# A long convolution beside a gated feed-forward layer: the convolution's transforms taken as two blocks of 1024 time steps

## The chip, the cores and the metric

The kernel runs on one core of one Trainium2 chip. The metric is the device time of one launch in microseconds (us). The engines are called PE (TensorE, matrix products), DVE (VectorE), ACT (ScalarE), POOL (GpSimd) and SP (SyncE, which here only issues DMAs).

## The reference

All inputs are bfloat16. `A_q`, `A_k`, `A_v` and the output are [1, 2048, 512] (time steps by channels), `ssm_k` is [512, 2048], `shift_k` [512, 4], the feed-forward weights are 512x1792, 512x1792 and 1792x512.

```python
def _A_ref(q, k, v, shift_k, ssm_k, ssm_D):
    ...                                   # k_shift: causal convolution of k with 4 taps for each channel
    kv = k_shift * v
    ...                                   # y: causal convolution of kv with ssm_k along time, 2048 steps, by FFTs of 4096
    y = y + kv * ssm_D[None, None, :]
    return q * y

def _B_ref(x, w_gate, w_up, w_down):
    h = _gelu(x @ w_gate) * (x @ w_up)
    return h @ w_down

x = A_q
xn = _layernorm(x, axis=-1)
s = _A_ref(xn, A_k, A_v, A_shift_k, A_ssm_k, A_ssm_D)
g = _silu(_B_ref(xn, B_w_gate, B_w_up, B_w_down))
return x + s * g
```

(`@` stands for the reference's einsums.)

## The kernel before

**Layout.** Partition p holds the time steps 16p to 16p+15; a tile t is one of the 16 steps, 128 partitions by 512 channels. The feed-forward part runs over four quarters q of four tiles. In a quarter, `unit(q, m)` computes for each of 14 chunks of 128 hidden columns four products for the gate (`g`) and four for the up projection (`u`), 512 wide, then Gelu on ACT (`GE`, L1072) and the product on DVE (`HT`, L1075). `down(q)` multiplies back: 14 products for each tile, in tasks of 4, 5 and 5; for quarters 0 to 2 the result becomes tanh-based silu in `G` (L1099, L1101), for quarter 3 it goes straight to the output (L1107 to L1110).

**The convolution.** It is done by transforms in several stages through DRAM scratch `ZH`, `ZK`, `ZI`:

- *First stage* (`stage1`, matrix `F1`): a transform along the 128 partitions. `x="H"` takes the filter `ssm_k` (transposed on PE before, `h_transpose`, L863; `ssm_D` is added to its first step), `x="K"` takes `kv` (in `V`). For each of the 16 tiles there are two products of 128 rows by 128 columns, 512 wide (real and imaginary part, `c`). Two such tiles go to one `AST` buffer (evicted by ACT or DVE, L593 or L596) and are stored to `ZH` or `ZK`.
- *Second stage* (`fwd`): the scratch is read back as 32 groups of 128 rows, four groups to a load of 512 KB (`BH`, `BK`). For each such load `tiles` issues 16 products of 32x32, at row and column positions 0, 32, 64 and 96, 512 wide, into four banks (L963). One is a "pass" below. H's results go to `HS`, and SP's swap DMAs make `HW` from it with even and odd partitions exchanged; K's go to `KB`.
- *Product and inverse* (`spectrum`): DVE multiplies `KB` into `HS` and `HW` in place (L1026, 1024 columns each, four for each load), and the inverse (`MI`) of the second stage is two passes that accumulate, one on `HS`, one on `HW`. The results go to `BO` and are stored to `ZI` from ACT's queue.
- *Last stage* (`y`): `ZI` is read back as 8 loads `BI`; for each there are four products with `G1`, 128 rows by 128 columns, 512 wide. DVE then multiplies with `XN` and `G` (L1146, L1152).

The matrices are made at the start from integer phases by the Sin function (L705), products of tables on DVE (L699, L702), sign changes on ACT (`m_turn`, L714) and three DMA transposes.

**Order.** All work is a list of tasks with numbers in the order in which `S.add` is called. `SEQ` is a written-out order of these numbers; a "b" behind a number takes the second engine offered (an eviction on DVE instead of ACT). `Sched.run` walks through `SEQ` and gives out buffers and PSUM banks by a model of durations; then each engine's instructions are issued in that order, and `Trk` puts in the semaphore waits. PSUM has 8 banks: `pF` gives out single banks to the feed-forward products (four at most), `pC` pairs of banks to the convolution. PE takes its products strictly in the order of `SEQ`.

The call for the small tiles, and the helper for the full ones:

```python
trk.op("PE", lambda h: h.matmul(ps(s, i)[b, :], lhsT=wt(col)[a, :], rhs=data(col)[a, :], start=n < 16, stop=n >= len(todo) - 16, tile_position=(32 * row, 32 * col)),
       r=rt, w=[R_ps[s][i]], accum=True, quiet=n < len(todo) - 1)

def mm(h, o, l, r, st, sp):
    return h.matmul(o, lhsT=l, rhs=r, start=st, stop=sp)
```

Of the kernel before, what the change touches and what calls it, by code (L numbers as in the profile page):

```python
# [6 lines left out]
BF16 = mybir.dt.bfloat16  # L7
# [7 lines left out]
DM = 512  # L15
# [5 lines left out]
NG = 32  # L21
# [34 lines left out]
T_INV = 438.0  # L56
# [335 lines left out]
def build_kernel(nc, A_q, A_k, A_v, A_shift_k, A_ssm_k, A_ssm_D, B_w_gate, B_w_up, B_w_down, out):  # L392
    with ExitStack() as es0:
# [23 lines left out]
        TFB = at("TFB", [128, NG, 32], BF16, place["at"] + 2048)  # L417
# [11 lines left out]
        SKB = new("SKB", [128, 4, DM], BF16)  # L429
        Drow = new("Drow", [1, DM], BF16)  # L430
# [22 lines left out]
        C32 = at("C32", [128, 2, 128], I32, xnT_at + 0)  # L453
        K32 = at("K32", [128, 128], I32, xnT_at + 1024)
        K4 = at("K4", [128, 128], I32, xnT_at + 1536)
# [9 lines left out]
        HW = [new(f"HW{j}", [128, 4, DM], BF16) for j in range(3)]  # L465
        HS.append(new("HS2", [128, 4, DM], BF16))
        KB = new("KB", [128, 4, 2, DM], BF16)
        BO = new("BO", [128, 4, 2, DM], BF16)
# [529 lines left out]
        for n in range(8):  # L998
            h_stage2(n)
# [222 lines left out]
```

## Time and profile before

| | |
|---|---|
| Median of 3 runs | 199.13 us (198.84 to 199.38) |
| Span of the profiled execution, first to last instruction | 197.8 us |
| PE busy | 191.3 us (97%), granted clock 0.999 |
| DVE, ACT, POOL busy | 161.5 us (82%), 119.5 us (60%), 12.2 us (6%) |
| PE products of the first stage: `V,F` and `HTr,F` | 32 and 32, 128\*128, 512 wide |
| PE products of the last stage: `BI,G` | 32, 128\*128, 512 wide |
| PE products of 32\*32: `BH`, `BK`, `HS`, `HW` | 128 each |
| DVE products of the spectrum (L1026) | 32 |

The span is the time between the first and the last instruction of one profiled execution; the time of a run is measured around it and is 1.3 us longer here. Durations of instructions overlap on an engine, so a product that is listed with 379 ns can start 216 ns after the one before it. In a line of groups the columns are line, engine, operation, out<-in, shape, count, then busy us and mean ns, then idle time before them and what ended it.

### The profile page before, as it was taken

The page shows a single profiled execution, that of the slowest core. Times are in us where ns is not written, and L with a number is a line of the kernel's source. Part 1 is how long each engine was busy: PE and PEld are TensorE (multiplying, and loading weights), DVE is VectorE, ACT ScalarE, POOL GpSimd, SP SyncE. Part 2 cuts the span into 40 slices and gives each one's busy share as a digit, 9 for nine tenths or more (in the row PEclk, how much of TensorE's full clock was granted, in tenths as well). Part 3 has the DMA queues.
Part 4 walks back from the last instruction along what each step waited for, and adds up shares of the span by engine and source line. Part 5 has one row for each costly group of instructions (what it writes and reads, how often), then busy time and mean ns, then how long its engine had stood idle before and what let it go on. Part 6 is the DMA issues. An engine that isn't in the chain of part 4 may idle for free.

```text
span 197.8 us, 3488 instructions
## 1 busy us (share of the span) xinstructions
PE 191.3 (97%) x1380; PEld 87.1 (44%) x1380; DVE 161.5 (82%) x247; ACT 119.5 (60%) x160; POOL 12.2 (6%) x26
## 2 busy tenths in 40 slices
PE   7989999899999999999999999999999999999993
PEld 2656644344444444443444333443344444444542
DVE  6687899888999898889589795897895765878994
ACT  4494877585978768875756958846754453330111
POOL 7300800000000000020200000000000000000000
PEclk9999999999999999999999999999999999999999
DMA  5999999999576849798999963994415133956363
GB/s 126 332 303 347 372 375 391 383 418 210 173 311 274 275 95 381 251 342 267 289 257 218 331 236 126 319 367 148 162 53 215 48 120 100 374 162 195 122 247 126
DMA packets 36870, 48.66 MB, mean 246 GB/s; under 512 B 10483, under 2 KB 29815, under 8 KB 36854
## 3 DMA queue, kind: packets, MB, share of 16 engines
q1 hardware_dynamic: 31350, 40.05, 64.0%
q10 hardware_dynamic: 5504, 8.39, 11.4%
q8 instruction: 11, 0.18, 0.4%
q14 instruction: 5, 0.04, 0.1%
HBM read 27.39 MB, written 14.68 MB: 213 GB/s over the span
## 4 chain that ended last, share of the span: by engine, by line
PE 89%; DMA 5%; SPq 2%; DVE 1%; issue 0%; ACT 0%
PE psall L602 83%; PE psall L963 5%; DMA Wu<-in_B_w_up_dram 5%; SPq L574 2%; PE psall L863 1%; DVE KTM L944 1%; DVE G L1109 0%; DVE G L1110 0%; ACT G L1107 0%
## 5 line engine op out<-in xcount | busy, mean ns | idle before, releaser
L602 PE MATMUL psall<-xnT,Wg 128*128 128x512 bf16 (+1 forms) x232 | 55.8, 372 | 1.7 <-DMA Wg<-in_B_w_gate_dram 1.0
L602 PE MATMUL psall<-xnT,Wu 128*128 128x512 bf16 (+1 forms) x232 | 55.3, 372 | 0.2 <-DMA Wu<-in_B_w_up_dram 0.2
L602 PE MATMUL psall<-Wd,HT 128*128 128x512 bf16 (+1 forms) x238 | 53.2, 367 | 0.0
L1075 DVE TENSOR_TENSOR HT<-psall,GE 128x512 bf16<-128x512 f32 x54 | 36.5, 686 | 10.1 <-PE psall L602 7.5
L1072 ACT ACTIVATE GE<-psall 128x512 bf16<-128x512 f32 x54 | 30.8, 599 | 14.0 <-PE psall L602 11.4
L602 PEld LDWEIGHTS psall<-xnT,Wg 128*128 128x128 bf16 x232 | 22.1, 98 | 27.6 <-ACT GE L1063 1.4
L602 PEld LDWEIGHTS psall<-Wd,HT 128*128 128x128 bf16 x238 | 22.6, 98 | 25.8 <-issue 1.9
L602 PEld LDWEIGHTS psall<-xnT,Wu 128*128 128x128 bf16 x232 | 21.8, 98 | 27.2 <-issue 2.2
L593 ACT ACTIVATE HS<-psall 128x1024 bf16<-128x1024 f32 x15 | 14.6, 1021 | 6.7 <-PE psall L963 6.7
L593 ACT ACTIVATE KB<-psall 128x1024 bf16<-128x1024 f32 x10 | 10.1, 1024 | 8.9 <-PE psall L963 8.9
L946 DVE TENSOR_TENSOR KAC<-KAC,KTM 128x2048 bf16<-128x2048 bf16 x12 | 14.6, 1218 | 0.1
L944 DVE TENSOR_TENSOR KTM<-KK,SKB 128x2048 bf16<-128x2048 bf16 x12 | 14.6, 1217 | 0.0
L593 ACT ACTIVATE AST<-psall 128x1024 bf16<-128x1024 f32 x12 | 11.9, 1022 | 2.5 <-PE psall L602 2.4
L596 DVE CAST BO<-psall 128x1024 bf16<-128x1024 f32 x7 | 8.6, 1223 | 5.6 <-PE psall L963 5.6
L1026 DVE TENSOR_TENSOR HS<-KB,HS 128x1024 bf16<-128x1024 bf16 x16 | 10.9, 684 | 1.6 <-ACT KB L593 1.6
L1099 ACT ACTIVATE G<-psall 128x512 bf16<-128x512 f32 x12 | 7.2, 601 | 8.2 <-PE psall L602 7.8
L1107 ACT ACTIVATE G<-psall 128x512 bf16<-128x512 f32 (+1 forms) x5 | 2.5, 511 | 15.9 <-PE psall L602 15.9
L593 ACT ACTIVATE BO<-psall 128x1024 bf16<-128x1024 f32 x9 | 9.1, 1024 | 4.8 <-PE psall L963 4.6
L806 DVE BATCH_NORM_STATS2 stats<-X 128x6 f32<-128x512 bf16 x16 | 10.5, 679 | 1.2 <-DMA X<-in_A_q_dram 1.0
L815 POOL TENSOR_TENSOR mv<-mv,NHALF 128x4 f32<-128x4 f32 (+1 forms) x5 | 5.9, 1176 | 83.8 <-DVE mv L814 83.8
L1026 DVE TENSOR_TENSOR HW<-KB,HW 128x1024 bf16<-128x1024 bf16 x16 | 10.9, 684 | 0.0
L596 DVE CAST KB<-psall 128x1024 bf16<-128x1024 f32 x6 | 7.3, 1223 | 3.6 <-PE psall L963 3.4
(79 smaller groups left out, 179.3 us busy)
## 6 DMA issues: line engine op xcount, KB each, us to landing
BH<-ZH SPq DMA_DIRECT2D x8, 512.0 KB, 5.1
HW<-HS SPq DMA_DIRECT2D x16, 256.0 KB, 3.8
BK<-ZK SPq DMA_DIRECT2D x8, 512.0 KB, 6.1
ZI<-BO ACTq DMA_DIRECT2D x16, 256.0 KB, 3.4
BI<-ZI SPq DMA_DIRECT2D x8, 512.0 KB, 4.5
ZK<-AST SPq DMA_DIRECT2D x6, 512.0 KB, 3.6
Hn<-in_A_ssm_k_dram SPq DMA_DIRECT2D x4, 512.0 KB, 7.9
KK<-in_A_k_dram SPq DMA_DIRECT2D x4, 512.0 KB, 11.9
```

What stands on the lines that cost most here:

```text
L593: return h.activation(o, i, ACTF.Copy, scale=scale)
L596: return h.tensor_copy(o, i)
L602: return h.matmul(o, lhsT=l, rhs=r, start=st, stop=sp)
L806: t_stats[t] = op([("DVE", 670.0)], lambda e, h, t=t: h.bn_stats(stats[:, t, :], X[:, t, :]), r=[bX[q][t % 4]], w=[bst[t]], rr=[R_X[t]], w ...
L815: t_pw = op([("POOL", 850.0)], lambda e, hd, ts=ts, n=n: hd.tensor_tensor(mv[:, ts, 3:4], mv[:, ts, 2:3], NHALF[:, 0:n, :], ALU.pow), r=[b ...
L944: op([("DVE", dur)], lambda e, h, j=j, m=m: h.tensor_tensor(KTM[:, m.slot, :, :], kk(j), sk(j), ALU.mult), r=need + [bSKB[j], a], w=[m], r ...
L946: op([("DVE", dur)], lambda e, h, m=m: h.tensor_tensor(KAC[:, a.slot, :, :], KAC[:, a.slot, :, :], KTM[:, m.slot, :, :], ALU.add), r=[m], ...
L963: trk.op("PE", lambda h: h.matmul(ps(s, i)[b, :], lhsT=wt(col)[a, :], rhs=data(col)[a, :], start=n < 16, stop=n >= len(todo) - 16, tile_po ...
L1026: return hd.tensor_tensor(o, flat(KB, kb[h]), o, ALU.mult)
L1072: op([("ACT", act(512))], lambda e, h: h.activation(GE[:, g.slot, :], bank(pg), ACTF.Gelu_apprx_tanh), r=[pg], w=[g], rr=lambda: R_bank(pg ...
L1075: op([("DVE", dve(512, 1))], lambda e, h: h.tensor_tensor(HT[:, q % 2, m, :], bank(pu), GE[:, g.slot, :], ALU.mult), r=[pu, g], w=[bHT[q][m]],
L1099: op([("ACT", act(n))], lambda e, h, g=g, pc=pc: h.activation(g, pc(), ACTF.Tanh, scale=0.5), r=[p], w=[bt], rr=lambda p=p: R_bank(p), ww= ...
```

## The change

The convolution of 2048 steps becomes one of two blocks of 1024 (`NB = 2`): block 0 of the output takes block 0 of both inputs; block 1 takes K's block 0 times the filter's second spectrum plus K's block 1 times the filter's first. Each block has 16 groups (`NG = 16`), so that the scratch has 32 groups as before.

- `F1` and `G1` shrink to [128, 128]. K's first stage is one task for two tiles with four products of 64 rows, at row positions 0 and 64. H's first stage has, for each tile, one product of the first 64 rows and one of all 128. The last stage is one task for two loads with eight products of 64 columns, at column positions 0 and 64.
- The forward passes stay 16. The inverses are four of two passes (block 0) and four of four passes (block 1).
- DVE's products of the spectrum are 12 for each pair of loads: four in place on the filter's second spectrum, four into `KB` buffers, four in place on its first; 48 in all.
- Scratch rows lie in runs of two tiles (2 KB) instead of four. The tables `TF`, `TFA`, `TFB`, `MI` have half the size. `HW` and `HS` have four buffers each, `KB` six, `BO` and the third `BK` lie elsewhere.
- `SEQ` is new as a whole. Of its entries, evictions on DVE: before, 7 of `BO`, 6 of `KB`, one of `HS`, one of `HTr`, two of `xnT`; after, 5 of `BO`, 2 of `KB`, two of `xnT`. The first loads on SP's queue: before `x0` (four), `h0`, `h1`, `wg0`, `x1`, `wg1`, `wu0`, the bulk of the halo of k, `h2`, `wu1`, `h3`; after `x0` (four), `h0`, `h1`, `wu0`, `wg0`, `x1`, `wg1`, the halo, `wu1`, `h3`, and `h2` five loads later. (`D0`, 1 KB, stands among the `x0`.)

Cut to its core, without `SEQ`, phases of the tables and pools:

```diff
-NG = 32
+NG = 16
+NB = 2
...
-        F1 = new("F1", [128, 2, 128], BF16)
-        G1 = new("G1", [128, 2, 128], BF16)
+        F1 = new("F1", [128, 128], BF16)
+        G1 = new("G1", [128, 128], BF16)
...
-        MI = new("MI", [128, 2, 8, 128], BF16)
+        MI = new("MI", [128, 2, NG // 4, 128], BF16)
         def stage1(x, u, Z):
             a = B(f"A{x}{u}", pAST[x])
             af = [] if x == "H" else s1_tasks["H"] + kshift_tasks[:1] + [t_table]
+            pp = [B(f"ps1{x}{u}_{i}", pC) for i in range(2)]
+            if x == "K":
+                def halves(e):
+                    for i in range(2):
+                        for b in range(2):
+                            k = slice(64 * b, 64 * b + 64)
+                            trk.op("PE", lambda h, i=i, b=b, k=k: h.matmul(ps(psl(pp[i]), b), lhsT=F1[k, :], rhs=V[k, 2 * u + i, :], start=True, stop=True, tile_position=(64 * b, 0)),
+                                   r=[R_F1, R_V[2 * u + i]], w=[R_ps[psl(pp[i])][b]], accum=True)
+                s1_tasks[x].append(S.add([("PE", 2 * T_FWD)], halves, r=[bF1, bKV[u // 2]], w=pp, lat=200.0, mode=2))
             for i in range(2):
-                p = B(f"ps1{x}{u}_{i}", pC)
+                p = pp[i]
                 data, rd, bd = (HTr[:, u, 512 * i:512 * i + 512], R_HTr[u], [bHTr[k][u // 4] for k in (2 * i, 2 * i + 1)] + ([bFold] if u == 0 else [])) if x == "H" else (V[:, 2 * u + i, :], R_V[2 * u + i], [bKV[u // 2]])
 
                 def m(e, p=p, data=data, rd=rd):
                     s = psl(p)
-                    for c in range(2):
-                        trk.op("PE", lambda h, c=c: mm(h, ps(s, c), F1[:, c, :], data, True, True), r=[R_F1, rd], w=[R_ps[s][c]], accum=True)
-                s1_tasks[x].append(S.add([("PE", pe(2))], m, r=[bF1] + bd, w=[p], lat=200.0))
+                    for b, k in ((0, 64), (1, 128)):
+                        trk.op("PE", lambda h, b=b, k=k: mm(h, ps(s, b), F1[0:k, :], data[0:k], True, True), r=[R_F1, rd], w=[R_ps[s][b]], accum=True)
+                if x == "H":
+                    s1_tasks[x].append(S.add([("PE", pe(2))], m, r=[bF1] + bd, w=[p], lat=200.0))
 
                 def ev(e, h, p=p, i=i):
                     if x == "K":
-                        return copy(e, h, ast[x][a.slot][:, i, :, :].rearrange("p c d -> p (c d)"), ps(psl(p)))
-                    return copy(e, h, ast[x][a.slot][:, :, :, 256 * i:256 * i + 256], ps(psl(p)).rearrange("p (c d r) -> p r c d", c=2, r=2))
+                        return copy(e, h, ast[x][a.slot][:, :, i, :], ps(psl(p)).rearrange("p (b d) -> p b d", b=2))
+                    return copy(e, h, ast[x][a.slot][:, :, :, 256 * i:256 * i + 256], ps(psl(p)).rearrange("p (b d r) -> p b r d", b=2, r=2))
                 op(EV(1024), ev, r=[p], w=[a], rr=lambda p=p: R_ps[psl(p)], ww=lambda: [R_AST[x][a.slot]], after=af)
 
             def st(e):
-                dst = bass.AP(Z, 4 * u * DM, [[32 * DM, 128], [DM, 4], [1, DM]])
-                dma(e, dst, ast[x][a.slot].rearrange("p r c d -> p (r c) d"), d_ast[x][a.slot], [R_AST[x][a.slot]], [R_Z[x][u]])
+                dst = bass.AP(Z, 2 * u * DM, [[16 * DM, 128], [NG * 128 * DM, NB], [DM, 2], [1, DM]])
+                dma(e, dst, ast[x][a.slot], d_ast[x][a.slot], [R_AST[x][a.slot]], [R_Z[x][u]])
             t_st = S.add([("ACT", 350.0) if x == "H" else ("SP", ISSUE)], st, r=[a], w=[bZ[x][u]], nbytes=1.9 * SMALL if x == "H" else W_ZK)
             (zh_tasks if x == "H" else zk_tasks).append(t_st)
 
...
-            return lambda e: tiles(pp, [(lambda c: TF[:, 4 * n + c, :], lambda c: T[:, buf.slot, c, :], [R_MF, R_T[buf.slot]])])
+            return lambda e: tiles(pp, [(lambda c: TF[:, 4 * (n % 4) + c, :], lambda c: T[:, buf.slot, c, :], [R_MF, R_T[buf.slot]])])
...
-        for out_ap, in_ap, rr, ww, rb, wb in ((G1[:], F1[:].rearrange("p c k -> p (c k)"), R_F1, R_G1, bF1, bG1), (MI[:, 0, :, :], TFA[:].rearrange("p g j -> p (g j)"), R_MFA, R_MI[0], bMF2, bMI[0]),
+        for out_ap, in_ap, rr, ww, rb, wb in ((G1[:], F1[:], R_F1, R_G1, bF1, bG1), (MI[:, 0, :, :], TFA[:].rearrange("p g j -> p (g j)"), R_MFA, R_MI[0], bMF2, bMI[0]),
...
-                op(EV(1024), lambda e, hd, p=p, h=h: copy(e, hd, HS[hs.slot][:, 2 * h:2 * h + 2, :].rearrange("p c d -> p (c d)"), ps(psl(p)), 2.0 ** -12),
-                   r=[p], w=[hs], rr=lambda p=p: R_ps[psl(p)], ww=lambda h=h: [R_HS[hs.slot][h]], after=g1_tasks + (kshift_tasks if n >= 2 else []))
+                op(EV(1024), lambda e, hd, p=p, h=h: copy(e, hd, HS[hs.slot][:, 2 * h:2 * h + 2, :].rearrange("p c d -> p (c d)"), ps(psl(p)), 2.0 ** -11),
+                   r=[p], w=[hs], rr=lambda p=p: R_ps[psl(p)], ww=lambda h=h: [R_HS[hs.slot][h]], after=g1_tasks + (kshift_tasks if n not in (0, 4) else []))
...
-        for n in range(8):
+        for n in (0, 4, 1, 5, 2, 6, 3, 7):
...
-        t_inv = []
...
-        def spectrum(n):
-            bk, hs, hw = B(f"bk{n}", pBK), bHS[n], bHW[n]
-            pk, pi = ([B(f"ps{x}{n}_{h}", pC) for h in range(2)] for x in "ki")
-            kb, bo = ([B(f"{x}{n}_{h}", p) for h in range(2)] for x, p in (("kb", pKB), ("bo", pBO)))
-            S.add([("SP", ISSUE)], lambda e: dma(e, BK[:, bk.slot, :, :], z_rows(ZK, 4 * n, 4), d_bk[bk.slot], R_Z["K"], [R_BK[bk.slot]]),
+        def kload(n):
+            bk = B(f"bk{n}", pBK)
+            S.add([("SP", ISSUE)], lambda e: dma(e, BK[bk.slot][:], z_rows(ZK, 4 * n, 4), d_bk[bk.slot], R_Z["K"], [R_BK[bk.slot]]),
...
-
-            S.add([("PE", T_FWD)], fwd(pk, BK, R_BK, bk, n), r=[bMF, bk], w=pk, lat=200.0, mode=1)
+            return bk
+
+        def kspec(n, bk):
+            pk, kb = ([B(f"{x}{n}_{h}", p) for h in range(2)] for x, p in (("psk", pC), ("kb", pKB)))
+            S.add([("PE", T_FWD)], lambda e: tiles(pk, [(lambda c: TF[:, 4 * (n % 4) + c, :], lambda c: BK[bk.slot][:, c, :], [R_MF, R_BK[bk.slot]])]), r=[bMF, bk], w=pk, lat=200.0, mode=1)
...
-                for b, T, R_o in ((hs, HS, lambda h=h: [R_HS[hs.slot][h]]), (hw, HW, lambda h=h: R_HW[hw.slot][h])):
-                    def mul(e, hd, h=h, b=b, T=T):
-                        o = T[b.slot][:, 2 * h:2 * h + 2, :].rearrange("p c d -> p (c d)")
-                        return hd.tensor_tensor(o, flat(KB, kb[h]), o, ALU.mult)
-                    op([("DVE", dve(1024, 2))], mul, r=[kb[h], hs, hw], w=[b], rr=lambda h=h, R_o=R_o: [R_KB[kb[h].slot]] + R_o(), ww=R_o)
+            return kb
+
+        def half(T, b, h):
+            return T[b.slot][:, 2 * h:2 * h + 2, :].rearrange("p c d -> p (c d)")
+
+        def inverse(s, b, terms):
+            n = 4 * b + s
+            pi, bo = ([B(f"{x}{n}_{h}", p) for h in range(2)] for x, p in (("psi", pC), ("bo", pBO)))
...
-                tiles(pi, [(lambda c, m=m: MI[:, m, n, 32 * c:32 * c + 32], lambda c, T=T, b=b: T[b.slot][:, c, :], [R_MI[m], *R_b])
-                           for m, T, b, R_b in ((0, HS, hs, R_HS[hs.slot]), (1, HW, hw, sum(R_HW[hw.slot], [])))])
-            t_inv.append(S.add([("PE", T_INV)], inv, r=[*bMI, hs, hw], w=pi, lat=200.0, mode=1))
+                tiles(pi, [(lambda c, m=m: MI[:, m, s, 32 * c:32 * c + 32], data, [R_MI[m], *rb()]) for m, data, rb, _ in terms])
+            S.add([("PE", T_FWD * len(terms))], inv, r=[*bMI, *[x for t in terms for x in t[3]]], w=pi, lat=200.0, mode=1)
...
-        for n in range(8):
-            spectrum(n)
+        def spectrum(s):
+            (h0, w0), (h1, w1) = ((bHS[n], bHW[n]) for n in (s, 4 + s))
+            bk0 = kload(s)
+            kb0 = kspec(s, bk0)
+            bt = [B(f"kt{s}_{h}", pKB) for h in range(2)]
+
+            def mul(h, kb, b, T, o, ob, R_i, R_o):
+                op([("DVE", dve(1024, 2))], lambda e, hd: hd.tensor_tensor(o(), flat(KB, kb[h]), half(T, b, h), ALU.mult), r=[kb[h], b, ob], w=[ob],
+                   rr=lambda: [R_KB[kb[h].slot]] + R_i(), ww=R_o)
+
+            def r_hs(b, h):
+                return lambda: [R_HS[b.slot][h]]
+
+            def r_hw(b, h):
+                return lambda: R_HW[b.slot][h]
+
+            def r_kb(b):
+                return lambda: [R_KB[b.slot]]
+
+            def in_place(kb, hs, hw):
+                for h in range(2):
+                    mul(h, kb, hs, HS, lambda h=h: half(HS, hs, h), hs, r_hs(hs, h), r_hs(hs, h))
+                    mul(h, kb, hw, HW, lambda h=h: half(HW, hw, h), hw, r_hw(hw, h), r_hw(hw, h))
+            in_place(kb0, h1, w1)
+            for h in range(2):
+                mul(h, kb0, h0, HS, lambda h=h: flat(KB, bt[h]), bt[h], r_hs(h0, h), r_kb(bt[h]))
+                mul(h, kb0, w0, HW, lambda h=h: flat(KB, kb0[h]), kb0[h], r_hw(w0, h), r_kb(kb0[h]))
+
+            def kb_term(m, b):
+                return m, lambda c: KB[:, b[c // 2].slot, c % 2, :], lambda: [R_KB[x.slot] for x in b], b
+
+            def h_term(m, T, b, R):
+                return m, lambda c: T[b.slot][:, c, :], R, [b]
+            inverse(s, 0, [kb_term(0, bt), kb_term(1, kb0)])
+            kb1 = kspec(4 + s, kload(4 + s))
+            in_place(kb1, h0, w0)
+            inverse(s, 1, [h_term(m, T, b, R) for hs, hw in ((h1, w1), (h0, w0))
+                           for m, T, b, R in ((0, HS, hs, lambda hs=hs: R_HS[hs.slot]), (1, HW, hw, lambda hw=hw: sum(R_HW[hw.slot], [])))])
+
+        for s in range(4):
+            spectrum(s)
...
+        p_y = [B(f"psy{j}", pC) for j in range(8)]
+        b_bi = [B(f"bi{j}", pBI) for j in range(8)]
...
-            p = B(f"psy{j}", pC)
-            bi = B(f"bi{j}", pBI)
+            p, bi = p_y[j], b_bi[j]
...
-                src = bass.AP(ZI, 4 * j * DM, [[32 * DM, 128], [DM, 4], [1, DM]])
-                dma(e, BI[:, bi.slot, :, :], src, d_bi[bi.slot], R_Z["I"], [R_BI[bi.slot]])
+                src = bass.AP(ZI, 2 * j * DM, [[16 * DM, 128], [NG * 128 * DM, NB], [DM, 2], [1, DM]])
+                dma(e, BI[:, bi.slot, :, :].rearrange("p (b t) d -> p b t d", b=NB), src, d_bi[bi.slot], R_Z["I"], [R_BI[bi.slot]])
...
-
-            def y(e, bi=bi, p=p):
-                s = psl(p)
-                for i in range(2):
-                    for c in range(2):
-                        trk.op("PE", lambda h, i=i, c=c: mm(h, ps(s, i), G1[:, c, :], BI[:, bi.slot, 2 * i + c, :], c == 0, c == 1),
-                               r=[R_G1, R_BI[bi.slot]], w=[R_ps[s][i]], accum=True)
-            S.add([("PE", pe(4))], y, r=[bG1, bi], w=[p], lat=200.0)
+            if j % 2 == 0:
+                continue
+
+            def y(e, j=j):
+                for jj in (j - 1, j):
+                    s, slot = psl(p_y[jj]), b_bi[jj].slot
+                    for i in range(2):
+                        for b in range(2):
+                            c = slice(64 * b, 64 * b + 64)
+                            trk.op("PE", lambda h, i=i, b=b, c=c, s=s, slot=slot: h.matmul(ps(s, i)[c, :], lhsT=G1[:, c], rhs=BI[:, slot, 2 * b + i, :], start=True, stop=True, tile_position=(0, 64 * b)),
+                                   r=[R_G1, R_BI[slot]], w=[R_ps[s][i]], accum=True)
+            S.add([("PE", 4 * T_FWD)], y, r=[bG1, *b_bi[j - 1:j + 1]], w=p_y[j - 1:j + 1], lat=200.0, mode=3)
+
+        for j in range(8):
+            p = p_y[j]
```

More of the change, by code (lines that the diff above doesn't have):

```diff
@@ L55 @@
 T_FWD = 219.0
-T_INV = 438.0
 N_HALF = 2
@@ L429, in build_kernel @@
         SKB = new("SKB", [128, 4, DM], BF16)
+        skb_at = place["at"] - 4 * DM * 2
         Drow = new("Drow", [1, DM], BF16)
@@ L464, in build_kernel @@
         place["at"] = kk_at + 2048
[L465 to L468, printed above, removed]
-        BK = new("BK", [128, 3, 4, DM], BF16)
-        assert place["at"] <= top
+        HW = [new(f"HW{j}", [128, 4, DM], BF16) for j in range(4)]
+        HS += [new(f"HS{j}", [128, 4, DM], BF16) for j in (2, 3)]
+        KB = new("KB", [128, 6, 2, DM], BF16)
+        BK = [new(f"BK{j}", [128, 4, DM], BF16) for j in range(2)]
+        BK.append(at("BK2", [128, 4, DM], BF16, skb_at))
+        assert place["at"] <= top, (place["at"], top)
+        BO = at("BO", [128, 4, 2, DM], BF16, ast_at)
         BI = at("BI", [128, 4, 4, DM], BF16, kk_at + 2048)
         ast = {"H": [T[:, 4 * j:4 * j + 4, :].rearrange("p (r c) d -> p r c d", c=2) for T in (XN, X) for j in (2, 3)], "K": [AST[:, j, :, :, :] for j in range(2)] + [ASX[:]]}
-        ZH = nc.dram_tensor("ZH", [NG, 128, DM], BF16, kind="Internal")
-        ZK = nc.dram_tensor("ZK", [NG, 128, DM], BF16, kind="Internal")
-        ZI = nc.dram_tensor("ZI", [NG, 128, DM], BF16, kind="Internal")
+        ZH = nc.dram_tensor("ZH", [NB * NG, 128, DM], BF16, kind="Internal")
+        ZK = nc.dram_tensor("ZK", [NB * NG, 128, DM], BF16, kind="Internal")
+        ZI = nc.dram_tensor("ZI", [NB * NG, 128, DM], BF16, kind="Internal")
         PSALL = es0.enter_context(nc.psum_tensor("psall", [128, 8 * 512], FP32))
@@ L538, in build_kernel @@
         R_BH = [res(f"BH{j}", BH[:, j, :, :]) for j in range(2)]
-        R_BK = [res(f"BK{j}", BK[:, j, :, :]) for j in range(3)]
+        R_BK = [res(f"BK{j}", T[:]) for j, T in enumerate(BK)]
         R_HS = [[res(f"HS{j}_{h}", T[:, 2 * h:2 * h + 2, :]) for h in range(2)] for j, T in enumerate(HS)]
@@ L545, in build_kernel @@
                 rh[1].ovl.remove(rh[0])
-        R_KB = [res(f"KB{j}", KB[:, j, :, :]) for j in range(4)]
+        R_KB = [res(f"KB{j}", KB[:, j, :, :]) for j in range(6)]
         R_BO = [res(f"BO{j}", BO[:, j, :, :]) for j in range(4)]
@@ L563, in build_kernel @@
         pBK = Pool_("BK", 3)
-        pKB = Pool_("KB", 4)
-        pHS = Pool_("HS", 3)
-        pHW = Pool_("HW", 3)
+        pKB = Pool_("KB", 6)
+        pHS = Pool_("HS", 4)
+        pHW = Pool_("HW", 4)
         pBO = Pool_("BO", 4)
@@ L680, in f_mul @@
             for c, off in ((0, float(TURN // 4 + TURN // 2)), (1, 0.0)):
-                PO(lambda h, c=c, off=off: h.tensor_scalar(C32[:, c, :], K4[:], Q32[:, 0:1], off, ALU.mult, ALU.add), [R_Q0, R_K4], [R_C32])
+                PO(lambda h, c=c, off=off: h.tensor_scalar(C32[:, :, c], K4[:], Q32[:, 0:1], off, ALU.mult, ALU.add), [R_Q0, R_K4], [R_C32])
         def f_phase():
@@ L719, in build_kernel @@
         S.add([("DVE", 360.0)], lambda e: f_phase(), r=[bFM], w=[bFP])
-        S.add([("ACT", 510.0)], lambda e: sin(F1, C32[:], [R_C32], R_F1), r=[bFP, bcq], w=[bF1])
+        S.add([("ACT", 510.0)], lambda e: sin(F1, C32[:].rearrange("p a c -> p (a c)"), [R_C32], R_F1), r=[bFP, bcq], w=[bF1])
         S.add([("DVE", 800.0)], lambda e: m_parts(), r=[bcq], w=[bQ])
@@ L726, in build_kernel @@
         for i in range(2):
-            S.add([("DVE", 1160.0)], lambda e, i=i: m_prod(i), r=[bTAB], w=[bTM[i]])
-        t_table = S.add([("DVE", 1160.0)], lambda e: m_sum(), r=bTM, w=[bMF])
+            S.add([("DVE", 690.0)], lambda e, i=i: m_prod(i), r=[bTAB], w=[bTM[i]])
+        t_table = S.add([("DVE", 690.0)], lambda e: m_sum(), r=bTM, w=[bMF])
         sin_tasks = [t_sin]
@@ L879, in build_kernel @@
         t_ln = ln(0)
-        S.add([("ACT", 2400.0)], m_turn, r=[bMF], w=[bMF2])
+        S.add([("ACT", 1900.0)], m_turn, r=[bMF], w=[bMF2])
         xn_transpose(0)
@@ L978, in build_kernel @@
         d_bh = [dsem(f"d_bh{j}") for j in range(2)]
-        d_hw = [[dsem(f"d_hw{j}_{c}") for c in range(2)] for j in range(3)]
+        d_hw = [[dsem(f"d_hw{j}_{c}") for c in range(2)] for j in range(4)]
         h2_tasks = []
```

22 lines of the change are left out of this document (11 added, 11 removed), and 42 rows, old and new, of the table SEQ.

## The prediction

> **What bounds the kernel now.** I read the busy shares first, then the chain that ended last, then the idle column of TensorE's groups, and last single stretches of the timeline.
>
> ```profile
> PE 191.3 (97%) x1380; PEld 87.1 (44%) x1380; DVE 161.5 (82%) x247; ACT 119.5 (60%) x160; POOL 12.2 (6%) x26
> ...
> PE 89%; DMA 5%; SPq 2%; DVE 1%; issue 0%; ACT 0%
> PE psall L602 83%; PE psall L963 5%; DMA Wu<-in_B_w_up_dram 5%; SPq L574 2%; PE psall L863 1%; DVE KTM L944 1%; DVE G L1109 0%; DVE G L1110 0%; ACT G L1107 0%
> ```
>
> TensorE (PE) is the bound: the chain is PE from 15.7 us to 193.4 us, but for one wait of VectorE. Full products start 216 ns apart. Summing starts over the trace, PE loses only 2.55 us to waits after its warm-up: 1.15 us and 0.40 us for the first gate and up weights, 0.90 us for a bank that VectorE, busy with the shift products, frees late, 0.1 us elsewhere:
>
> ```profile
> 14.45 1.02 PE L602 MATMUL psall<-xnT,Wg 128*128 128x512 bf16 x4 [0.98 <-DMA Wg<-in_B_w_gate_dram]
> 15.71 1.03 PE L602 MATMUL psall<-xnT,Wu 128*128 128x256 bf16 x8 [0.23 <-DMA Wu<-in_B_w_up_dram]
> ```
>
> (The bracket is the idle time before; the start-to-start loss is 0.16 us more.) So what the change does to PE's own stream is what it does to the time, up to 2.5 us of waits that could still go and any new ones.
>
> **Prices from the trace.** Small tiles of 32x32 run sixteen at once; the timeline shows a visit to them between full products:
>
> ```profile
> 82.72 1.03 PE L602 MATMUL psall<-xnT,Wu 128*128 128x512 bf16 x4
> 83.67 0.43 PE L963 MATMUL psall<-BH,TF 32*32 32x512 bf16 x16
> 84.04 1.04 PE L602 MATMUL psall<-xnT,Wu 128*128 128x512 bf16 x4
> 84.92 0.59 PE L602 MATMUL psall<-xnT,Wg 128*128 128x512 bf16 x2
> ```
>
> ```profile
> 103.55 0.43 PE L963 MATMUL psall<-HS,MI 32*32 32x512 bf16 x16
> 103.78 0.42 PE L963 MATMUL psall<-HW,MI 32*32 32x512 bf16 x16
> ```
>
> From 82.72 to 84.92 is 2.20 us for eight full products (8 x 0.216 = 1.73) and one pass of tiles: 0.47 us, of which 0.216 is the pass. The visit thus costs 0.254 us beyond its work. By single starts that is 93 ns to get in (309 instead of 216), 50 ns in which the sixteen tiles start 3 ns apart, 101 ns to get out (317; 90 when two passes run), 10 ns on the product after. Without the sixteen starts a visit costs 0.204 us, or 0.193 with several passes. A second pass starts 0.227 us after the first (103.55 to 103.78).
>
> **The change on PE, part by part.**
>
> 1. First stage of K (`halves`): 32 full products become 16 pairs of 64-row products at row positions 0 and 64, 8 tasks of two pairs. If a pair takes one slot, 16 x 0.216 = 3.46 us go. That a pair overlaps is not shown for 64 rows; the row above it shows four row groups and four column groups overlapping, so I take the slot, and the other bound is no gain.
> 2. Last stage (`y`): 32 full products become 16 pairs of 64-column products, 4 tasks of four pairs: again 3.46 us go.
> 3. Inverse: eight visits of two passes become four of two and four of four: 8 x 0.227 = +1.82 us. The sixteen forward passes stay.
> 4. Visits. I numbered the tasks of both versions in the order in which they are added and read both `SEQ` strings by it. Before there are 24 visits, each alone between full products. After there are 24 of 32x32, 8 of K and 4 of y, none next to another: 12 x 0.193 = +2.32 us, and 11 ns for each of 20 later passes, +0.22.
> 5. First stage of H: still 32 products, but every first one of a pair now has 64 rows (`F1[0:64]`). The call names no tile, but the 32x32 calls name no size either, only a position, and the profile shows them as 32*32: the size follows the operands. So I expect 64*128 there, alone between two full products: 16 more visits x 0.204 = +3.26 us. Bounds: nothing (no switch of mode), and 0.25 us each (+4.0) at the price of the visit shown; I take 0.204, the same row less its sixteen starts.
>
> Sum on PE: -6.91 + 1.82 + 2.32 + 0.22 + 3.26 = +0.71 us. What the half-array pairs save is eaten by 28 more visits.
>
> On part 5 the Trainium skill speaks too: TensorEngine Tiling (Array Packing), section Key Properties, says that changing the tiling mode, not just the tile, drains TensorE. The rows agree for 32*32 (0.204 us a visit); no row here shows 64*128. By that rule part 5 stands at +3.26 and the sum at +0.71; if it spared 64 rows at position 0, the sum would be -2.55.
>
> **Beside PE.** VectorE: 32 spectrum products become 48. Its eviction entries in `SEQ` (suffix b) go from 14 of 1024 columns and one of the H transposes to 7, and three table products halve:
>
> ```profile
> L596 DVE CAST BO<-psall 128x1024 bf16<-128x1024 f32 x7 | 8.6, 1223 | 5.6 <-PE psall L963 5.6
> L1026 DVE TENSOR_TENSOR HS<-KB,HS 128x1024 bf16<-128x1024 bf16 x16 | 10.9, 684 | 1.6 <-ACT KB L593 1.6
> ```
>
> By start-to-start times (0.60 a product, 1.14 an eviction): 16 x 0.60 = +9.6, 7 x 1.14 = -8.0, the H one -0.6, tables 3 x 0.5 = -1.5: about -0.5 us, hidden behind PE as before. ScalarE takes the evictions: 8 x 1.02 = +8.2 us, less about 1.5 of `m_turn` at half size; 119.5 becomes about 126 of 198, hidden by PE; the cover fails only where several evictions stand in a row.
>
> DMA: `ZH`, `ZK` and `ZI` have runs of 2 KB in place of 4. In the trace a 4 KB packet takes 159 ns and a 2 KB one 84, so 2048 stored packets become 4096: 18 us over 16 engines, 1.2 us of each, spread over 27 to 90 us. Nothing on PE's chain waits for a store; K's loads before the first K pass landed at 91.5 us for a pass at 94.0, and 2 us of that margin are used up by the new order. I take nothing, bound +0.6.
>
> Start: on SP's queue the up weights of the first chunk now stand ahead of the gate's, `x1` and the second gate chunk behind both. Landings before: second H load 9.3, first gate 10.0, `x1` 12.0, second gate 14.3, first up 15.6. With 256 KB more ahead of it (1536 KB at 1280 KB in 5.0 us) the second gate lands at 15.3, and PE comes to it at 14.2 (its order summed at the prices above, plus the start): a wait of 1.1 in place of 1.15 + 0.40, so -0.45 us. The 0.90 us for VectorE: it has 1.5 us less table work ahead and PE comes later by the visits of part 5; I take half, -0.45, between -0.9 and 0. A new wait of as much again is possible.
>
> End: the last y task (j=0 and 1) now stands 15 full and 24 half-width products before PE's end, 5.9 us. VectorE has two instructions of 1.14 and two of 0.60 for it, 3.5 us, then the gating of the last three tiles, which comes about 0.2 us later than the products allow: +0.2.
>
> Total: 197.8 + 0.71 - 0.45 - 0.45 + 0.2 = 197.8 us span. The profiled execution stands 1.3 us below the median 199.13 of the runs, which I add: **199.1 us, no change to be told**. A measurement of this kernel tells some 0.3% (0.6 us) from no change.
>
> **The rivals.**
>
> - *The 64-row products of H cost no switch.* For: no tile is named, and position 0 is the full array's. Against: the sizes in the profile. Then 3.26 us go; but PE would reach the first products of the second quarter at about 50.7 us, and their transposed input landed at 52.6 before, so up to 1.8 come back. 199.1 - 3.26 + 0.9 = 196.8. Chance 0.14.
> - *Slower: PE waits for VectorE's products at the last inverses.* An inverse of the second block needs eight products in place of four. In `SEQ`, from the last K pass to the last inverse stand 17 VectorE instructions, 17 x 0.60 = 10.2 us, against 11.6 us of PE; to the inverse before, five (3.0) against 3.1. It decides when VectorE enters this stretch more than 0.1 to 1.4 us late. For: from 60 to 84 us it was 90% busy. Against: between 130 and 160 us it was 22.8 of 30, and after 36 us PE lost only 0.1 us to any wait. Price 1 to 3 us: 201.1. Chance 0.17.
> - *The pairs do not overlap.* Then 6.91 us come back: 206.0. The 3 ns between tile starts speak against it: 0.04.
> - *The sum as worked out*: 0.62, by itself 197.9 to 200.3 (part 5 at 0.15 to 0.25 us a visit, the waits between -1.3 and +0.6). Something else 0.03.
>
> **How the numbers follow.** Within the likeliest case I give 0.33 to more than 0.6 us faster, 0.38 within, 0.29 slower. Faster: 0.62 x 0.33 + 0.14 x 0.95 = 0.34, and 0.01. Same: 0.62 x 0.38 + 0.01 = 0.25. Slower: 0.62 x 0.29 + 0.17 x 0.95 + 0.04 + 0.02 = 0.40. The range takes in the first rival and most of the second, 196.2 to 201.8; about 0.05 lies below and 0.10 above.
>
> **What would show it.** `V,F` at 64*128, 32 products in 16 near-simultaneous starts, its visits at some 0.63 us between the full products beside them where four products took 0.86; `BI,G` at 128*64 likewise, 4 visits of about 1.08; inverse visits of 64 tiles at about 1.16. `HTr,F` in two forms, 16 at 64*128 and 16 at 128*128, with starts of 309 and 317 ns around the former; 216 there means the first rival. PE busy and without waits after 36 us; an idle PE with VectorE's KB, HS or HW as releaser ahead of an inverse means the second. The forecast is wrong if new waits pass 1 us in sum, or if a 64-row visit costs far from 0.2 us.

## The result and the profile after

The changed kernel takes 201.88 us (median of 4 runs, 201.74 to 202.25) against 198.99 us for the kernel before on the same chip: ratio 1.0139, 95% interval 1.01 to 1.0177. That is slower by 2.8 us, where 199.1 and no change were predicted, and 0.08 us above the top of the range. The profiled execution has a span of 200.1 us (197.8 before); in it PE's last product starts at 196.59 us, in that of before at 194.21.

The page of the changed kernel, busy shares and the chain of work that ended last:

```profile
PE 189.9 (95%) x1493; PEld 83.1 (42%) x1508; DVE 162.0 (81%) x255; ACT 126.0 (63%) x168; POOL 12.1 (6%) x26
...
PE 71%; DMA 15%; ACT 4%; DVE 3%; issue 2%; SPq 2%; POOL 1%; ACTq 0%; DVEq 0%
PE psall L604 61%; DMA ZH<-XN 6%; PE psall L975 6%; DMA X<-in_A_q_dram 4%; DMA BK<-ZK 4%; PE psall L1198 2%; SPq L576 2%; PE psall L899 2%; DMA ZK<-AST 1%; DVE stats L808 1%; ACT AST L595 1%; ACT HTr L595 1%; ACT XN L595 1%; PE psall L865 1%; ACT KB L595 1%
```

PE is still the engine with the most work, ScalarE grew to the 126 us forecast, and VectorE has 0.5 us more instead of 0.5 less. But the chain before was 89% PE; now a quarter of it is transfers, evictions and issues. So not only the work on PE has changed: PE waits for others. The groups of PE by shape (busy us, mean ns, idle before) show the new forms:

```profile
L604 PE MATMUL psall<-HTr,F 64*128 64x512 bf16 x16 | 6.2, 387 | 1.8 <-ACT HTr L595 1.8
L604 PE MATMUL psall<-HTr,F 128*128 128x512 bf16 x13 | 5.1, 390 | 0.0
L899 PE MATMUL psall<-V,F 64*128 64x512 bf16 x32 | 4.8, 381 | 0.1
...
L1198 PE MATMUL psall<-BI,G 128*64 128x512 bf16 x32 | 4.2, 385 | 0.0
```

H's first stage has its two forms, 16 products at 64\*128 (of the 16 at 128\*128 three are missing from the trace). What they cost is read from PE's timeline (start, duration, and idle time before in the bracket):

```profile
17.60 1.03 PE L604 MATMUL psall<-xnT,Wg 128*128 128x512 bf16 x4 [0.16 <-DVE XN L820]
18.56 0.71 PE L604 MATMUL psall<-HTr,F 64*128 64x512 bf16 x2
19.11 2.33 PE L604 MATMUL psall<-xnT,Wu 128*128 128x256 bf16 x12
21.27 0.60 PE L865 MATMUL psall<-ident,Hn 128*128 128x128 f32 x4
22.99 0.71 PE L604 MATMUL psall<-HTr,F 64*128 64x512 bf16 x2 [1.12 <-ACT HTr L595]
...
28.28 0.39 PE L604 MATMUL psall<-HTr,F 64*128 64x512 bf16 x1 [0.67 <-ACT HTr L595]
...
73.20 1.03 PE L604 MATMUL psall<-xnT,Wg 128*128 128x512 bf16 x4
74.16 0.61 PE L899 MATMUL psall<-V,F 64*128 64x512 bf16 x4
74.70 1.04 PE L604 MATMUL psall<-xnT,Wu 128*128 128x512 bf16 x4
75.57 1.03 PE L604 MATMUL psall<-Wd,HT 128*128 128x512 bf16 x4
```

From 17.60 to 19.11 are six products (the two `HTr,F` are one of each form) in 1.51 us instead of 6 x 0.216 = 1.30: the lone product of 64 rows costs 0.21 us more than its slot. From 73.20 to 75.57 are eight full products and one K visit, 2.37 - 1.73 = 0.64 us for four products of 64 rows, where before four full ones took 0.86. Both prices are close to the forecast ones (0.204 and 0.63 us). What is new are the brackets at 22.99 and 28.28: PE stands still behind ScalarE's evictions of the H transposes. PE's waits over the whole span:

```profile
PE psall L604 <- DMA Wg<-in_B_w_gate_dram: 1.8, 1, 1.8
PE psall L604 <- ACT HTr L595: 1.8, 2, 1.1
PE psall L604 <- DVE Q L689: 1.2, 1, 1.2
PE psall L604 <- issue: 0.9, 6, 0.2
PE psall L975 <- DMA BK<-ZK: 0.5, 1, 0.5
```

(`Q` is a wait in the warm-up, as long before. Most of the "issue" stands beside the missing records.) By starts, as in the prediction (how much later a product starts than its slot allows), the waits for `Wg`, `HTr` and `BK` are losses of 1.97, 1.93 and 0.62 us.

### The profile page after: what moved, and what is told of

Same layout as the page of the kernel before. It is cut to its first block, busy times and chain, and to the rows that moved or that the text cites. A ratio compares the mean times of both kernels' runs of the same rounds, so it can differ in the third digit from the quotient of the medians.

```text
span 200.1 us, 3742 instructions
## 1 busy us (share of the span) xinstructions
PE 189.9 (95%) x1493; PEld 83.1 (42%) x1508; DVE 162.0 (81%) x255; ACT 126.0 (63%) x168; POOL 12.1 (6%) x26
## 4 chain that ended last, share of the span: by engine, by line
PE 71%; DMA 15%; ACT 4%; DVE 3%; issue 2%; SPq 2%; POOL 1%; ACTq 0%; DVEq 0%
PE psall L604 61%; DMA ZH<-XN 6%; PE psall L975 6%; DMA X<-in_A_q_dram 4%; DMA BK<-ZK 4%; PE psall L1198 2%; SPq L576 2%; PE psall L899 2%; DMA ZK<-AST 1%; DVE stats L808 1%; ACT AST L595 1%; ACT HTr L595 1%; ACT XN L595 1%; PE psall L865 1%; ACT KB L595 1%
## 5 line engine op out<-in xcount | busy, mean ns | idle before, releaser
L604 PE MATMUL psall<-Wd,HT 128*128 128x512 bf16 (+1 forms) x226 | 50.1, 366 | 0.9 <-issue 0.6
L1125 ACT ACTIVATE GE<-psall 128x512 bf16<-128x512 f32 x54 | 31.7, 600 | 21.0 <-PE psall L604 17.9
L595 ACT ACTIVATE HS<-psall 128x1024 bf16<-128x1024 f32 x16 | 15.7, 1022 | 6.1 <-PE psall L975 5.9
L595 ACT ACTIVATE KB<-psall 128x1024 bf16<-128x1024 f32 x14 | 13.8, 1025 | 3.2 <-PE psall L604 1.9
L595 ACT ACTIVATE BO<-psall 128x1024 bf16<-128x1024 f32 x11 | 11.2, 1024 | 6.2 <-PE psall L975 6.0
L1154 DVE SCALAR_TENSOR_TENSOR G<-G,psall 128x512 bf16<-128x512 bf16 x12 | 7.9, 683 | 7.3 <-ACT G L1152 7.3
L604 PE MATMUL psall<-HTr,F 64*128 64x512 bf16 (+1 forms) x29 | 10.2, 388 | 1.8 <-ACT HTr L595 1.8
L595 ACT ACTIVATE X<-psall 128x1024 bf16<-128x1024 f32 x8 | 8.2, 1024 | 4.3 <-PE psall L604 4.2
```

What stands on the lines that cost most here:

```text
L595: return h.activation(o, i, ACTF.Copy, scale=scale)
L1125: op([("ACT", act(512))], lambda e, h: h.activation(GE[:, g.slot, :], bank(pg), ACTF.Gelu_apprx_tanh), r=[pg], w=[g], rr=lambda: R_bank(pg ...
L1154: op([("DVE", dve(512, 1))], lambda e, h, g=g, pc=pc: h.scalar_tensor_tensor(out=g, in0=g, scalar=1.0, in1=pc(), op0=ALU.add, op1=ALU.mult ...
```

## Experiments

The main question: is the loss PE's own work, above all the mode switches of H's products, or is it the waits? The ratios are to the kernel before on the same chip. "Stores on SP" moves four stores of `ZH` to SyncE's queue, "V earlier" one load of V; both are explained below.

| kernel | median us | ratio, 95% interval |
|---|---|---|
| changed kernel | 201.88 | 1.0139 [1.01, 1.0177] |
| H's first products on 128 rows | 200.15 | 1.0035 [1.0002, 1.0068] |
| H-transpose resource split | 199.94 | 1.0042 [1.0012, 1.0073] |
| both | 209.5 | none |
| second gate chunk loaded earlier | 201.88 | 1.0134 [1.0061, 1.0207] |
| kernel before, H's first products on 64 rows | 201.71 | 1.013 [1.0079, 1.0181] |
| both, stores on SP, V earlier | 197.87 | 0.996 [0.993, 0.9991] |
| both, stores on SP | 197.48 | 0.9923 [0.9887, 0.9958] |
| both, V earlier | 209.19 | 1.0496 [1.0424, 1.0568] |
| kernel before, stores on SP | 199.84 | 1.0055 [1.0014, 1.0096] |
| changed kernel, stores on SP | 201.22 | 1.0117 [1.0071, 1.0163] |
| resource split, stores on SP | 199.14 | 1.0001 [0.9975, 1.0027] |

**H's first products on 128 rows.** `FZ` is `F1` with zeros in its second 64 rows (a memset on DVE, a copy on ACT), so that no mode changes there:

```diff
-                    for b, k in ((0, 64), (1, 128)):
-                        trk.op("PE", lambda h, b=b, k=k: mm(h, ps(s, b), F1[0:k, :], data[0:k], True, True), r=[R_F1, rd], w=[R_ps[s][b]], accum=True)
+                    for b, F, R_F in ((0, FZ, R_FZ), (1, F1, [R_F1])):
+                        trk.op("PE", lambda h, b=b, F=F: mm(h, ps(s, b), F[:], data, True, True), r=[*R_F, rd], w=[R_ps[s][b]], accum=True)
```

> The changed kernel with H's 64-row products taken away: the first block's matrix stands once more with zeros in rows 64 to 127, and H's first stage takes 128 rows in both products, so that its 16 switches of mode go. Theory A (PE's own stream and its waits add up to the time): 16 visits at 0.20 us go, 201.9 - 3.3 = 198.6 us, HTr,F all 128*128 with starts 216 ns apart. Theory B (a chain through memory sets the time in the middle: stores of ZH, the transposed input of quarter 1 landing at 52.6 us, stores of ZK, the load of BK before the first K pass at 96 us): PE arrives earlier and waits there, 2 us or more come back, 200.6 us or above, with waits on DMA after 48 us.

Measured: 200.15 us, by the ratios 1.0139 - 1.0035 = 1.04%, 2.1 us less than the changed kernel, between the two theories. The switches are worth 3.3 us (16 x 0.208); over a microsecond of it comes back as a wait where there was none, for the transposed input of the second quarter (1.2 us by starts). PE's timeline:

```profile
53.86 1.89 PE L606 MATMUL psall<-xnT,Wg 128*128 128x512 bf16 x8 [1.04 <-DMA xnT<-XN]
```

**The resource of the H transposes, split.** A row `HTr[:, t, :]` was one resource to `Trk` (the unit for which it keeps who writes and who reads), although a first-stage product reads half of its columns, those of two of the four transposes. So a product of the first half had to wait for the evictions of the second half that `SEQ` had put ahead of it:

```diff
-        R_HTr = [res(f"HTr{t}", HTr[:, t, :]) for t in range(NT // 2)]
+        R_HTr = [[res(f"HTr{t}_{i}", HTr[:, t, 512 * i:512 * i + 512]) for i in range(2)] for t in range(NT // 2)]
...
-                   rr=lambda hf=hf: R_bank(pp[hf]), ww=R_HTr[4 * hf:4 * hf + 4]))
+                   rr=lambda hf=hf: R_bank(pp[hf]), ww=[r[k // 2] for r in R_HTr[4 * hf:4 * hf + 4]]))
```

> The changed kernel with one thing else: the waits on HTr are kept for each half of its columns, so that H's first products (columns of k 0 and 1) no longer wait for the evictions of k 2 and 3. Theory A: the two waits of PE at 21.6 and 27.3 us (1.19 and 0.74 us) go and stay away, 201.9 - 1.9 = 200.0 us. Theory B: they come back at 50 to 96 us, 201.3 us or above.

Measured: 199.94 us, by the ratios 0.97% or 1.9 us less than the changed kernel, as much as the two waits, which are gone from PE's waits. That the numbers agree so well is partly luck: between the two profiled executions other pieces moved too and about cancel, the start and the gate wait together by -0.8 us and the wait for `BK` by -0.4, a wait for `BH` and the one for `KB` by +0.5 each. PE's timeline at the same place:

```profile
20.57 0.60 PE L865 MATMUL psall<-ident,Hn 128*128 128x128 f32 x4
21.11 0.71 PE L604 MATMUL psall<-HTr,F 64*128 64x512 bf16 x2
21.65 1.03 PE L604 MATMUL psall<-xnT,Wg 128*128 128x512 bf16 x4
```

The product stands right behind the transposes, with no bracket. The wait was thus not for data; the order of work alone would not have made it, nor the coarse resource under the old order, where the trace has no such wait.

**Both edits.**

> Both of the edits before. Theory A: 201.9 - 3.3 - 1.9 = 196.7 us, below the kernel before. Theory B: PE is 5 us earlier at the same landings, most comes back, 199.5 us or above.

Measured: 209.5 us (204.47 to 212.22 in four runs, too far apart for a ratio): theory A fails by 12.8 us, and theory B, which gave only a lower bound, does not account for the 10 us above it. The lowest of the four runs is still slower than the changed kernel; the profiled one took 210.9 us. PE's timeline, and below it SyncE's queue:

```profile
51.74 0.70 PE L902 MATMUL psall<-V,F 64*128 64x512 bf16 x4 [3.20 <-DVE V L963]
52.38 2.32 PE L606 MATMUL psall<-Wd,HT 128*128 128x512 bf16 x5
60.32 3.57 PE L606 MATMUL psall<-xnT,Wg 128*128 128x512 bf16 x8 [5.62 <-DMA xnT<-XN]
```

```profile
36.52 13.78 SPq L836 DMA_TRANSPOSE xnT<-XN  x1
```

The transposed input of the second quarter lands at 60.2 us; in the changed kernel it landed at 52.6, in the two single edits at 53.7 and 53.2. The last four stores of `ZH` were issued at 48.4 to 54.6 us in the changed kernel, at 45.7 to 52.5 in the single edits, and at 42.9 to 48.6 here, while transposes and loads of V are under way. The idea to test: PE is early, so the stores are early, and they hold up what PE needs next.

**The stores moved, and a load moved.** Three kernels with both edits: the last four stores on SP's queue, where they stand behind the transpose; V's second load one step earlier in SP's order; and both. The first of these edits:

```diff
-            t_st = S.add([("ACT", 350.0) if x == "H" else ("SP", ISSUE)], st, r=[a], w=[bZ[x][u]], nbytes=1.9 * SMALL if x == "H" else W_ZK)
+            t_st = S.add([("ACT", 350.0) if x == "H" and u in (2, 4, 6, 7) else ("SP", ISSUE)], st, r=[a], w=[bZ[x][u]], nbytes=1.9 * SMALL if x == "H" else W_ZK)
```

> Both edits of the run before (H in 128 rows, waits on HTr by halves), and two on memory: the last four stores of ZH are issued from SP's queue, where they stand behind the transposed input of quarter 1, and the load of V's second quarter stands ahead of the third. Theory C (as PE gets earlier the stores of ZH come earlier too and take bandwidth from the loads and the transpose in front of quarter 1, which then land later): the transpose lands at 52 us or before instead of 60.2, the waits of 6.0 and 3.3 us go, 196.5 to 198.5 us. Theory B alone (loads are simply not there earlier whatever the stores do): 52.5 us of landing against 48.5 of PE, 4 us of waits and a slower clock after it, 200 us or above.

> As that, without the earlier load of V. Theory C: the transpose lands near 52 us, the wait for V (3.3 us, landing at 50) stays: 199 to 201 us. Theory B: 203 us or above, as with both edits alone.

> As that, with the earlier load of V and the stores where they were. Theory C: the wait for V goes, the transpose still lands near 60 us and PE waits more than 6 us for it: 203 us or above. Theory B: the same. If V alone held everything up: 197 to 199 us.

Measured: with the stores moved 197.48 us, with the load moved 209.19, with both 197.87. It is the stores; the load moved earlier brings no gain. With the load moved, the transpose lands at 59.3 us and PE waits 7.93 us for it, so the late landing is there in a second profile. The expectation for the stores alone, 199 to 201 us, was missed: V's load landed at 48.6 us instead of 50.3, and of the wait of 3.20 us for V 1.24 stayed. SyncE's queue with the stores moved, and PE at the second quarter:

```profile
35.84 12.46 SPq L836 DMA_TRANSPOSE xnT<-XN  x1
49.61 1.09 SPq L578 DMA_DIRECT2D ZH<-X  x2
50.75 2.17 SPq L578 DMA_DIRECT2D ZH<-XN  x2
```

```profile
50.10 0.61 PE L902 MATMUL psall<-V,F 64*128 64x512 bf16 x4 [1.24 <-DVE V L963]
51.73 1.89 PE L606 MATMUL psall<-xnT,Wg 128*128 128x512 bf16 x8
```

The transpose is issued 0.7 us earlier than with both edits alone, but lands at 50.4 instead of 60.2, before any of the four stores has landed (the first lands at 52.6). This kernel is faster than both kernels of the study, than the one before by 0.8%: 0.9923 [0.9887, 0.9958].

**Is it the stores by themselves?** The same move of stores in the kernel before, in the changed kernel, and with the split resource alone:

> The kernel before, with four of the eight stores of ZH (the last four in the order of work) issued from SyncE's queue, behind the transpose of the second quarter's input, in place of ScalarE's. Theory A (the stores matter only where TensorE comes early to the second quarter, as it does once the H-transpose waits and the mode switches are gone): in the kernel before TensorE loses 0.1 us to waits after 36 us, the transpose may land some 2 us earlier but nobody waits for it; 198.7 to 199.7 us, ratio 1.000 within 0.4%. Theory B (the move is a gain of its own, so that what the kernel with all three edits gained over before is not the change's): 197.5 us, ratio 0.992.

> The changed kernel with the same four stores on SyncE's queue, H's products on 64 rows and the tracker as changed. Theory A: TensorE comes to the second quarter when the transpose has landed already, so no wait goes there; 201.3 to 202.0 us, at most 0.6 us less through the first load of BK. Theory B: about 200.2 us, 1.7 less.

> The changed kernel with the H-transpose resource split in column halves and the four stores on SyncE's queue; H's products stay on 64 rows. Against the kernel with all three edits (197.5 us) it has the 16 mode switches (3.3 us), but TensorE comes later to what it waited for there (2.2 us of waits, of which I take 1 to go). Theory A: 199.3 to 200.0 us, that is nothing or 0.4 us less than with the split tracker alone (199.9), since TensorE reached the second quarter at 53.1 there and the transpose had landed at 53.2. Theory B (the stores cost more than that one wait): 198.2 us or less.

Measured: 199.84 us (ratio 1.0055), 201.22 (1.0117) and 199.14 (1.0001). In the kernel before the move gains nothing and rather loses, a little more than theory A's 0.4%: its profiled execution has a wait for `GE` (0.5 us) that the other has not; why is open. In the changed kernel it gives 0.2%, within the intervals. With the split resource it gives 0.4%, 0.8 us, more than the 0 to 0.4 of theory A, less than theory B's: the waits there for `BH` (0.5) and most of that for `KB` (0.6) went. With the stores on SP, the split resource is worth 1.0117 - 1.0001 = 1.2% (2.3 us) and H on 128 rows a further 0.8% (1.6 us, half of the switches). So the 1.5 us by which the best kernel beats the one before are not the stores' own: they come out once the new waits and the switches are gone, and the stores keep the memory from taking them back.

**H's first products on 64 rows in the kernel before** (the real part thus leaves out half of the filter):

```diff
-                        trk.op("PE", lambda h, c=c: mm(h, ps(s, c), F1[:, c, :], data, True, True), r=[R_F1, rd], w=[R_ps[s][c]], accum=True)
+                        trk.op("PE", lambda h, c=c: mm(h, ps(s, c), *((F1[0:64, 0, :], data[0:64]) if x == "H" and c == 0 else (F1[:, c, :], data)), True, True), r=[R_F1, rd], w=[R_ps[s][c]], accum=True)
```

> The kernel before, with one thing else: of H's first-stage products the first of each pair takes rows 0 to 63 alone (its output leaves out half of the filter's real part), so that the 16 switches of mode come in with nothing else of the change. Theory A (PE's stream adds up): 16 x 0.20 = +3.3 us, of which the wait of 0.90 us at 34.6 us may take up a part: ratio to before 1.012 to 1.017. Theory B (the middle waits for memory, and PE's own time before 50 us does not count): PE there has xnT of quarter 1 at 52.6 us and reaches it at 54, so nothing to take it up, the same ratio; below 1.006 only if the switch is cheaper than in the profile of the changed kernel.

Measured: 201.71 us, ratio 1.013 [1.0079, 1.0181], 2.6 us more: 16 switches at 0.208 us are 3.3, less the 0.90 us for VectorE's `KTM`, which is gone from its waits, makes 2.4. PE's timeline of it has the price once more:

```profile
26.44 1.03 PE L602 MATMUL psall<-xnT,Wu 128*128 128x512 bf16 x4
27.40 0.71 PE L602 MATMUL psall<-HTr,F 64*128 64x512 bf16 x2
27.95 1.89 PE L602 MATMUL psall<-xnT,Wg 128*128 128x512 bf16 x8
```

Six products in 27.95 - 26.44 = 1.51 us again. No row of the kernel before showed this mode; the Trainium skill's rule that a change of tiling mode drains TensorE (TensorEngine Tiling (Array Packing), section Key Properties) agrees with this row: 0.208 us, without any tile position named.

**The second gate chunk loaded earlier** (in `SEQ`, the entries of `x1` and of this chunk exchanged, `37 22` to `22 37`):

> The changed kernel with two neighbours on SP's queue exchanged: the second gate chunk before x1. It should land near 12.8 us instead of 15.1. Theory A: PE's wait of 1.97 us at 13.2 us goes, less what the second up chunk (landing at 18.0) gives back, 200.0 to 200.9 us. Theory B: no gain, 201.5 us or above.

Measured: 201.88 us, 1.0134 [1.0061, 1.0207], no gain, as in theory B. The chunk lands at 11.95 us and the wait of 1.97 us for it is gone. But in this profiled execution PE's first transpose of H starts 1.08 us later, and a wait of 0.97 us for VectorE's `HT` (idle 0.80 us before the product at 17.35 us) is new; the two waits for the evictions of the H transposes are as long as in the changed kernel.

## Why the prediction was wrong

**PE's own stream: right.** In brackets is what the prediction's terms give. K's first stage: 8 x (0.634 + 0.010 - 0.864) = -1.76 us (-1.82), where the 10 ns are what the product behind a visit starts late. Last stage: 4 x (1.080 + 0.010 - 1.728) = -2.55 (-2.55). Inverses: 4 x 1.162 + 4 x 0.676 - 8 x 0.676 = +1.94 (+1.82). H: 16 x 0.208 = +3.33 (+3.26). The sum is +0.96 against +0.71 forecast; the whole stream without waits grew by 1.0 us. The rest is under 0.1 us, with 15 matmul records missing.

**Start: right in sum by luck, not in its parts.** The gate chunk landed at 15.1 us (15.3 forecast), but PE's warm-up ended 0.88 us earlier than in the run before, which was not foreseen: the wait was 1.97 us, not 1.1, and start and wait together gave -0.46 (-0.45). When the first transpose of H starts differs between runs of one order, 7.48 us in the profile of the changed kernel and 8.81 in the one with stores on SP, and the wait at the gate chunk differs against it (1.97 and 0.85). The traces show what it follows: the 22 warm-up products start 427 ns apart at first and 216 ns apart later, from 6.2 us in the profile of the kernel before, 4.5 in that of the changed kernel and 6.7 in the one with stores on SP. So the 0.88 us belong to the execution and not to the change. Taking the wait away by the earlier load gained nothing.

**VectorE's late bank: under-sized.** The wait of 0.90 us went wholly, where I took half.

**New waits: the step that failed.** "A new wait of as much again is possible" stood in the text, and the sum put it at nothing. There are three: 1.93 us at the evictions of the H transposes, 0.62 us at the first load of `BK`, and 0.24 us for a bank that ScalarE frees with an eviction to `KB`, before the product at 132.3 us; 2.8 us together. The condition that the prediction set for being wrong, new waits over 1 us in sum, came true. The largest could be read from the two texts on hand: the new order puts first-stage products right behind the transposes of the other column half, and `R_HTr` is one resource for the whole row. I had compared the orders for visits and for loads, not for what stands just ahead of each product's resource. The split resource shows it: with it both waits at the H transposes are gone, and the time falls by 1.9 us.

**DMA: the bound was the value.** I took nothing for K's loads and wrote down +0.6 as the bound. PE's timeline has it:

```profile
96.67 0.44 PE L975 MATMUL psall<-BK,TF 32*32 32x512 bf16 x16 [0.54 <-DMA BK<-ZK]
```

The load landed at 96.6 (91.5 before) for a pass that could have run 0.6 us earlier. A margin of 2.5 us of which the order uses up 2 is no margin. Nor is it a fixed cost: with H's products on 128 rows alone PE was earlier and still idle for 0.57 us there, while with both edits and stores on SP `BK` landed at 91.8 for a pass at 91.85.

**End.** -0.1 us instead of +0.2. **Sum:** +1.0 - 0.46 - 0.90 + 1.93 + 0.62 + 0.24 - 0.1 = +2.3 us, the 197.8 and 200.1 of the spans. The profiled run took 201.92 us, 1.8 around its span, where I had added 1.3; that is the other 0.5 us of the miss. In every run for which both are on record, of the kernel before too, the time stands 1.75 to 1.87 us above the span, and the spans of the kernel before range from 195.8 to 198.4 us. So the 1.3 us was no property of the kernel: the time of the profiled execution of 197.8 us is not on record, but by this it was about 199.6 us, 0.5 above the median that it was set against.

**The rivals.** The products of H do cost a switch (chance 0.14 for none), and that without them up to 1.8 us would come back at the second quarter's input was right in kind: 1.2 us did. The pairs overlap. The slower rival named a time near the result, 201.1, but a cause that did not occur: ahead of the inverses PE has no wait for VectorE's products. That cases of slowing by other waits had only 0.03 is the second fault: an order of some 770 tasks, all new, has more places for a wait than the one that I worked out.

## What to carry to other kernels

When a written-out order is replaced, look in it, for each product on the bounding engine, at what was queued last on the resources that it waits for, as the tracker cuts them and not as the data are; and when a margin shrinks to some tenths, price the wait. A matmul with fewer rows than its neighbours (64 here, beside 128) was not a smaller one but a change of mode: in a stream of full products give it the full rows with zeros, or put products of one mode together (the second was not tried here). And when waits are taken off the bounding engine, ask what it sets off earlier: here the stores came into the loads that it needed next, and only moving them kept the gain.

## What the runs showed of the hardware

The last four `ZH` stores, issued 2.7 to 4.6 us earlier than in either single edit, put the landing of one DMA transpose from 53.2 or 53.7 us to 60.2, with PE idle for two stretches, and the four kernels with both edits show that it is the stores (60.2 and 59.3 with them early, 50.4 and 51.65 with them behind the transpose). Whether it is their time or their queue that matters was not separated, since the move changes both.

The idle time then costs twice. Busy time of each engine from 53 to 62 us (PE, its loads, DVE, ACT, POOL, then granted clock, DMA share and GB/s), first with both edits, then with the stores moved too:

```profile
53.00:62.00 9.00, 3.38 (x9) 0.90 (x8) 4.37 (x4) 1.24 (x2) 0.00 (x0) 0.50 1.06 310
```

```profile
53.00:62.00 9.00, 9.00 (x45) 3.58 (x44) 8.97 (x11) 7.07 (x12) 0.00 (x0) 1.00 1.01 338
```

The granted clock is 0.50 from 53 to 62 us, and the eight products from 60.32 us take 3.57 us where eight took 1.89 elsewhere. The kernel with both edits and the load of V moved, idle for 7.93 us, shows the same: 0.50 from 57 to 62 us, and 3.57 us for the eight products. The Trainium skill (TensorE: Matmul & The Clock Gate, section What's actually happening) says that an idle window of some 3.4 us puts the clock at half. The traces agree with the half, 0.50; the clock was already down to 0.66 on average from 51.7 to 53 us, behind an idle time of 3.20 us, a little under that figure, and with idle times up to 1.24 us (stores moved) it stayed at 1.00.
